# A conv-and-softmax-layer kernel: the prologue written anew, its first tiles in pairs, the tail's rows last

## The chip, the cores and the metric

The kernel runs on one core of a Trainium2 chip. The metric is the device time of one execution in microseconds (us). Engines: PE (TensorE: matmuls), PEld (its weight loads), ACT (ScalarE), DVE (VectorE), POOL (GpSimd), SP (SyncE, which here issues every DMA).

## The reference

```python
# x (8, 4160, 192), weight (8 heads, 7 taps); D = 192, 24 columns to a head
w = exp(weight - max(weight)); w = w / (sum(w) + 1e-9)
y[b, s, h, :] = sum_k w[h, k] * x[b, s + k - 6, h, :]      # zero before the start
# y as 33280 tokens of 192; w_in (192, 1024), w_out (1024, 192) are float64, g_ln (1024)
h = y @ w_in
e = exp(h - max(h)); sm = e / (sum(e) + 1e-9)
solu = h * sm
ln = (solu - mean(solu)) / sqrt(var(solu) + 1e-6) * g_ln
out = ln @ w_out
```

## The kernel before

Everything is one stream of 260 tiles of 128 tokens. x comes in 17 chunks (`Chunk`, L113): chunk 0 has 1024 rows (tiles 0 to 7), chunk 1 the other 1056 of the first half sequence (tiles 8 to 15), chunk 2 and the rest 2080 each. A chunk is loaded in windows of 112 rows with 16 of halo. PE convolves groups of heads with a banded tap matrix (`product`, L240, tiles pc), ACT and DVE write the result as two fp16 parts (`upper`, L293, `lower`, L302, tile y), SP turns them with transposing DMAs (`turn`, L335, y to yT), and `double` (L345) copies a third of yT to y2. A chunk has a power-of-two scale s, from squares that are summed (`sum_squares`, L164, tiles xj and xa), added over the partitions by a small PE matmul (`add_up`, L201) and turned into a power of two by four small DVE steps (`root_power`, L90). The scale's columns cv follow in `scale_steps` (L182).

A tile t then takes these steps: h in PSUM by ten matmuls 512 wide, yT against high and low parts of w_in (`emit_rows` L740, `emit_third` L748; two banks ph in rotation); its maximum on DVE (L772); exp on ACT (L779); the product e times h on DVE (L832, `emit_mul`, which frees ph); the fp16 high part on ACT (L840), the low part on POOL (L849), both transposed by one DMA (L851, pT); a square sum on ACT (L844); and, five tiles later, 24 matmuls 192 wide against ohi and olo, w_out's parts (L861, po), which DVE copies out (L868). For groups of up to eight tiles POOL makes the reciprocal roots (L912 to L922), the rows are multiplied by them on DVE or POOL (L931, L927, `run_rows` L1074), and SP stores pairs of rows (L940). The last three tiles are groups of one: a root of small steps each (L875 to L879) and the output straight from PSUM (L884, of).

The weights come as float64 words and are decoded by hand (`Words`, L483 on): exponent bits (L498) and mantissa bits (L503) cut on DVE, mantissa and low word joined to a float (L530 for w_in on DVE; L509, L521 and L524 for w_out on ACT and POOL), the exponent turned to a power of two on ACT (L536, `powers`), the sign put in on DVE (L539), and both multiplied (L546). w_in is worked on in two halves of 512 columns and a third part Z, the last 64 rows laid on all partitions. Its scale t_in is found from the largest absolute value (L515) and goes into the bias of `powers`, so that all later steps depend on it. whi is cast on ACT (L625, L643 to L648), wlo is the rest on DVE (L634). w_out's values are multiplied by g_ln and the powers in eight DVE steps (L695), its mean over the rows is made on PE (L704) and taken off on DVE (L714), ohi is cast on ACT (L718) and olo made on DVE (L723).

Each engine works its instructions off in the order in which the code issues them; nothing is reordered. What follows what is set by hand: `step(i)` (L1217) issues one tile and the parts of its neighbours, for tiles 0 to 7 and the last ones; `two_steps(i)` (L1146) issues a pair, for tiles 8 to 255. `chores` (L978) says, by fractions of a chunk's tiles, at which tile the next chunks are convolved (conv), opened, turned, doubled, loaded and summed. A run of matmuls of tile t + 2 waits until `emit_mul` of tile t has freed its buffer in PSUM.

## Time and profile before

| | us |
|---|---|
| median of three runs | 1205.08 (1202.68 to 1205.13) |
| the profiled execution | 1204.79 |
| its span in the trace | 1203.1 |
| PE busy in the span | 1158.8 (96%) |
| DVE, ACT, POOL busy | 1009.3, 946.3, 946.6 |
| start of tile 2, tile 8, tile 18 on PE | 37.47, 80.96, 137.72 |
| last instruction on an engine (L884) | 1199.98 |

A row of a timeline gives start, duration, engine, line, operation, output and inputs, and in brackets how long the engine stood idle before it and what ended that. A tail of "x2" says that two like instructions run together in one row, with the time from the first's start to the last's end. A row of the waits gives the total, the number and the longest. A row by lines gives busy time and mean ns of one.

### The profile page before, as it was taken

Reading aid. Unit: us, or ns where it says so; the run is one execution under the profiler, and the core shown is the slowest. Engines: PE = TensorE matmul, PEld = TensorE weight load, DVE = VectorE, ACT = ScalarE, POOL = GpSimd, SP = SyncE. Lnnn points to the kernel's source line nnn. Section 1 sums busy time; section 2 is a strip of 40 time slices with the busy share of each in tenths; the row PEclk is TensorE's granted clock in tenths of the full one; section 3 lists DMA queues with packets and bytes.
Section 4 is the critical chain, followed back from the end, with each engine's and each line's share of the span. In section 5 each row is a group of like instructions: output and inputs, shape, how many; then the busy total and the mean of one; then the engine's idle time right before and its main releaser. Section 6 shows DMA issues by size and latency. Waiting matters only on the chain.

```text
span 1203.1 us, 26422 instructions
## 1 busy us (share of the span) xinstructions
PE 1158.8 (96%) x9718; PEld 815.8 (68%) x9718; DVE 1009.3 (84%) x2172; ACT 946.3 (79%) x1518; POOL 946.6 (79%) x920
## 2 busy tenths in 40 slices
...
GB/s 246 96 168 127 164 207 193 211 201 202 209 193 208 187 211 197 202 196 185 217 175 218 179 199 208 194 200 185 213 205 206 194 189 155 170 171 191 183 156 153
DMA packets 727312, 227.48 MB, mean 189 GB/s; under 512 B 651454, under 2 KB 725582, under 8 KB 727182
## 3 DMA queue, kind: packets, MB, share of 16 engines
...
## 4 chain that ended last, share of the span: by engine, by line
PE 75%; POOL 8%; DVE 7%; issue 6%; ACT 2%; DMA 1%; POOLq 0%; ACTq 0%; SPq 0%; DVEq 0%
PE po L861 33%; PE ph L740 31%; POOL p L849 6%; PE pc L270 5%; PE ph L748 5%; DVE ph L772 1%; DVE e L832 1%; DMA yT<-y 1%; POOL t L921 1%; POOL raw L927 1%; ACT e L779 1%; DVE y L306 1%; DVE xa L171 0%; ACT y L297 0%; DMA pT<-p 0%
## 5 line engine op out<-in xcount | busy, mean ns | idle before, releaser
L849 POOL TENSOR_TENSOR p<-e,p 128x1024 f16<-128x1024 f32 x257 | 546.3, 2135 | 187.7 <-ACT p L840 187.6
L861 PE MATMUL po<-ohi,pT 128*128 128x192 f16 x4160 | 553.6, 246 | 4.3 <-DVE raw L931 4.3
L861 PEld LDWEIGHTS <-pT 128*128 128x128 f16 x6240 | 522.3, 98 | 37.9 <-DMA pT<-p 5.0
L861 PE MATMUL po<-olo,pT 128*128 128x192 f16 x2080 | 512.4, 246 | 1.5 <-DVE olo L723 1.5
L740 PE MATMUL ph<-whi,yT 128*128 128x512 f16 x1560 | 430.0, 385 | 21.2 <-DVE e L832 12.1
L779 ACT ACTIVATE e<-ph,sm 128x1024 f32<-128x1024 f32 x259 | 288.7, 1115 | 195.4 <-DVE ph L772 178.8
L772 DVE TENSOR_SCALAR_CACHE_REDUCE ph<-ph,cv 128x1024 f32<-128x1024 f32 x248 | 318.8, 1290 | 140.0 <-PE ph L748 92.3
L740 PEld LDWEIGHTS <-yT 128*128 128x128 f16 x2080 | 192.2, 99 | 271.3 <-issue 71.4
L832 DVE SCALAR_TENSOR_TENSOR e<-ph,cv,e 128x1024 f32<-128x1024 f32 x247 | 316.3, 1281 | 3.2 <-ACT e L779 1.3
L840 ACT CAST p<-e 128x1024 f16<-128x1024 f32 x259 | 269.5, 1040 | 21.3 <-DVE e L832 21.2
L844 ACT ACTIVATE sq<-e 128x1024 f32<-128x1024 f32 x259 | 273.7, 1057 | 3.9
L740 PE MATMUL ph<-wlo,yT 128*128 128x512 f16 x520 | 157.1, 384 | 2.5 <-DVE wlo L634 2.5
L225 POOL TENSOR_TENSOR xs<-xr,xs 128x960 f16<-128x960 f32 (+1 forms) x56 | 107.8, 1925 | 2.3
L868 DVE COPY raw<-po 128x192 f32<-128x192 f32 x257 | 90.6, 352 | 1.3 <-PE po L861 1.3
L306 DVE SCALAR_TENSOR_TENSOR y<-pc,y 112x480 f16<-112x480 f32 (+3 forms) x168 | 74.5, 471 | 17.0 <-ACT y L297 9.8
L748 PE MATMUL ph<-wlo,yT 64*128 64x512 f16 x268 | 82.8, 388 | 0.0
L748 PE MATMUL ph<-wlo,y 64*128 64x512 f16 x252 | 77.1, 385 | 0.0
L270 PE MATMUL pc<-xs,taps_hi 128*112 128x240 f16 (+1 forms) x448 | 72.9, 261 | 0.0
L171 DVE TENSOR_REDUCE xa<-xr 128x1 f32<-128x384 f32 x120 | 69.3, 618 | 0.0
L297 ACT ACTIVATE y<-pc 112x432 f16<-112x432 f32 (+5 forms) x140 | 63.3, 473 | 1.7 <-PE pc L270 0.6
L222 POOL TENSOR_SCALAR xr<-xr,s 128x960 f32<-128x960 f32 (+1 forms) x56 | 57.7, 1030 | 2.6 <-ACT xs L216 0.4
L270 PE MATMUL pc<-xs,taps_lo 128*112 128x240 f16 (+1 forms) x224 | 58.5, 261 | 0.0
...
## 6 DMA issues: line engine op xcount, KB each, us to landing
out_dram<-raw SPq DMA_DIRECT2D x128, 192.0 KB, 2.5
...
pT<-p SPq DMA_TRANSPOSE x259, 4.9
...
yT<-y SPq DMA_TRANSPOSE x99, 3.7
...
```

The source lines that it names most:

```text
L225: (2.1 * size + 0.2, lambda: pool.tensor_tensor(xl, r, h, ALU.subtract)),
L270: nc.tensor.matmul(o, tp[:, h + j, :], r, start=q == 0, stop=q == len(ops) - 1)
L740: nc.tensor.matmul(bank, lhs, w[:, r, n * 512 : (n + 1) * 512], start=start and j == 0, stop=stop and j == len(ops) - 1,)
L748: nc.tensor.matmul(banks_of(t)[n], y[q, t.off : t.off + P], wlo[q, 1, n * 512 : (n + 1) * 512], start=start, stop=not start,)
L772: dve.tensor_scalar(t.ph, t.ph, t.cv[:, 0:1], None, ALU.mult, ALU.min, accum_out=t.bias)
L779: act.activation(t.e, t.ph, AF.Exp, bias=t.bias, scale=-1.0, accum_out=grp.z[:, g : g + 1])
L832: dve.scalar_tensor_tensor(t.e, t.ph, t.cv[:, 3:4], t.e, ALU.mult, ALU.mult, accum_out=t.grp.s1[:, t.g : t.g + 1],)
L840: act.copy(t.p16[:, :, 0, :], t.halves)
L844: act.activation(junk, t.e, AF.Square, accum_out=t.grp.s2[:, t.g : t.g + 1])
L849: eng.tensor_tensor(t.p16[:, :, 1, :], t.halves, t.p16[:, :, 0, :], ALU.subtract)
L861: nc.tensor.matmul(t.po[:, 0:D], t.pT[:, a, :], w, start=j == 0, stop=j == len(ops) - 1)
L868: dve.tensor_copy(t.grp.raw[:, t.g, :], t.po[:, 0:D])
```

## The change

It has five parts. Lines of the changed kernel are shifted: `root_power` stays, L740 becomes L729, L772 L764, L832 L824, L849 L841, L851 L843, L931 L923.

w_in: its exponents become powers of two with a fixed bias, with no scale; ACT squares the powers and sums them (`squares`), PE adds the sums up, and t_in is made from that. Signs and values are done without t_in, which is applied where whi is copied (ACT, scale=t_in) and where wlo is made (DVE). `largest`, `floor`, `iq` and `bias_in` are gone. This is ACT in the prologue, before, where the powers of w_in and then whi wait on bias_in:

```order
12 L536 ACTIVATE e_in<-e_in,bias_in 128x512 x2
13 L297 ACTIVATE y_0_0_175<-pr_223,s_172 112x5x96
14 L297 ACTIVATE y_0_0_175<-pr_224,s_172 112x5x32
15 L297 ACTIVATE y_0_0_175<-pr_224,s_172 112x5x64
16 L625 CAST whi<-f_in 128x512 x2
17 L536 ACTIVATE e_in<-e_in,bias_in 128x512
18 L509 ACTIVATE raw_out<-raw_out 128x1536
19 L643 CAST whi<-f_in 64x512
20 L644 CAST whi<-f_in 64x512
21 L647 CAST whi<-f_in 64x512
22 L648 CAST whi<-f_in 64x512
```

and after, with rebias in place of bias_in, the squares at L464, and t_in among the inputs of whi:

```order
8 L177 ACTIVATE xj_2_169,xa_132<-xr_1_88 128x384
9 L481 ACTIVATE e_in<-e_in,rebias 128x512
10 L177 ACTIVATE xj_3_172,xa_132<-xr_1_88 128x576
11 L464 ACTIVATE oj_in_191,isq<-e_in 128x1024
12 L481 ACTIVATE e_in<-e_in,rebias 128x512
13 L305 ACTIVATE y_0_0_180<-pq,s_177 112x5x96
14 L305 ACTIVATE y_0_0_180<-pq,s_177 112x5x32
15 L305 ACTIVATE y_0_0_180<-pq,s_177 112x5x64
16 L464 ACTIVATE oj_in_209,isq<-e_in 128x512
17 L305 ACTIVATE y_0_0_180<-pr_219,s_177 112x5x96
18 L627 ACTIVATE whi<-f_in,t_in 128x512 x2
19 L635 ACTIVATE whi<-f_in,t_in 64x512 x4
```

The powers of w_in stand ahead of the first y rows of chunk 0 now (those of the first half two rows ahead of this piece), and the six copies of whi follow each other behind the scale.

w_out: the lows, the cast of the mantissas and the last product go to POOL, the factor g_ln to ACT (eight scalings of 192 columns), half of olo to POOL; t_out is in the averaging matrix `even` and in the subtraction of the mean. POOL before, from the end of its memsets on:

```order
15 L410 MEMSET even 128x128
16 L524 TENSOR_TENSOR f_out<-m_out,raw_out 128x1536
17 L849 TENSOR_TENSOR p_1_401<-e_338,p_1_401 128x2x512
18 L849 TENSOR_TENSOR p_2_446<-e_421,p_2_446 128x2x512
19 L849 TENSOR_TENSOR p_3_514<-e_443,p_3_514 128x2x512
20 L849 TENSOR_TENSOR p_4_581<-e_511,p_4_581 128x2x512
```

and after; raw_out, m_out, f_out and e_out are w_out's words, mantissas, values and powers:

```order
14 L416 MEMSET even 128x128
15 L450 TENSOR_SCALAR raw_out<-raw_out 128x1536
16 L198 TENSOR_SCALAR cv_178<-cv_178 128x1 x2
17 L456 TENSOR_SCALAR m_out<-m_out 128x1536
18 L469 TENSOR_TENSOR f_out<-m_out,raw_out 128x1536
19 L491 TENSOR_TENSOR f_out<-f_out,e_out 128x1536
20 L841 TENSOR_TENSOR p_0_322<-e_305,p_0_322 128x2x512
21 L841 TENSOR_TENSOR p_1_342<-e_320,p_1_342 128x2x512
22 L714 TENSOR_TENSOR olo<-f_out,ohi 128x768
23 L841 TENSOR_TENSOR p_2_409<-e_396,p_2_409 128x2x512
```

Five instructions for w_out stand where one stood, and the low halves begin with tile 0, which DVE made before.

Tiles 0 to 7 go in pairs: `first_two`, `second_two`, then `two_steps` from tile 4. Chunk 1's first two groups are convolved beside tiles 2 and 3 and kept (`early`), its sums of squares come behind tile 3's cast, and chunk 2's four first sums are squares on ACT.

Chunk 1 and 2 in `chores`: chunk 1's groups at tiles 4 and 5, chunk 2's groups one or two a pair over tiles 8 to 19, where they were two a pair over tiles 8 to 15. Chunk 2's transposes on SP, before, with y_2_0 its first ten windows:

```order
41 L851 DMA_TRANSPOSE pT_913<-p_10_910 128x16x128
42 L851 DMA_TRANSPOSE pT_923<-p_11_918 128x16x128
43 L336 DMA_TRANSPOSE yT_942<-y_2_0_751 128x10x112 x2
44 L150 DMA xr_1_973<-in_x_dram 128x5x192
45 L851 DMA_TRANSPOSE pT_1049<-p_12_1046 128x16x128
46 L851 DMA_TRANSPOSE pT_1063<-p_13_1054 128x16x128
47 L336 DMA_TRANSPOSE yT_942<-y_2_0_751 128x10x112
48 L349 DMA y_2_943<-yT_942 64x1120
49 L150 DMA xr_2_1112<-in_x_dram 128x5x192
```

and after:

```order
39 L843 DMA_TRANSPOSE pT_905<-p_10_902 128x16x128
40 L843 DMA_TRANSPOSE pT_915<-p_11_910 128x16x128
41 L150 DMA xr_1_947<-in_x_dram 128x5x192
42 L843 DMA_TRANSPOSE pT_1016<-p_12_1013 128x16x128
43 L843 DMA_TRANSPOSE pT_1027<-p_13_1022 128x16x128
44 L344 DMA_TRANSPOSE yT_1041<-y_2_0_757 128x10x112 x3
45 L357 DMA y_2_1042<-yT_1041 64x1120
46 L150 DMA xr_2_1083<-in_x_dram 128x5x192
```

All three transposes of its first ten windows follow pT of tile 13 now, where two stood one pair earlier.

The tail: `run_rows` is left out at tiles 257 to 259, so that rows of the groups at tile 240 and 248 are multiplied behind the last low parts (pl), and stores behind the last transposes. DVE before, with raw_15626 the rows of tiles 248 on and raw_15853 those of 252 on:

```order
1428 L931 TENSOR_SCALAR raw_15626,t_248_15318<-raw_15626,t_248_15319 128x192 x4
1429 L832 SCALAR_TENSOR_TENSOR e_15881,s_258_15862<-ph_15866,cv_13211,e_15881 128x1024
1430 L772 TENSOR_SCALAR ph_15929,sm_15943<-ph_15929,cv_13211 128x1024
1431 L868 COPY raw_15853<-po_15950 128x192
1432 L849 TENSOR_TENSOR p_258_15941<-e_15881,p_258_15941 128x2x512
1433 L800 SCALAR_TENSOR_TENSOR el_15945<-ph_15929,cv_13211,el_15945 128x512
1434 L800 SCALAR_TENSOR_TENSOR el_15946<-ph_15929,cv_13211,el_15946 128x512
1435 L808 TENSOR_TENSOR pl_15983<-el_15945,pl_15983 128x512
1436 L808 TENSOR_TENSOR pl_15986<-el_15946,pl_15986 128x512
1437 L931 TENSOR_SCALAR raw_15853,t_252_15531<-raw_15853,t_252_15532 128x192 x3
```

and after, where raw_15198 is tile 240's group, raw_15624 248's and raw_15851 252's:

```order
1384 L860 COPY raw_15851<-po_15936 128x192
1385 L841 TENSOR_TENSOR p_258_15927<-e_15873,p_258_15927 128x2x512
1386 L792 SCALAR_TENSOR_TENSOR el_15931<-ph_15915,cv_13209,el_15931 128x512
1387 L792 SCALAR_TENSOR_TENSOR el_15932<-ph_15915,cv_13209,el_15932 128x512
1388 L800 TENSOR_TENSOR pl_15969<-el_15931,pl_15969 128x512
1389 L800 TENSOR_TENSOR pl_15972<-el_15932,pl_15972 128x512
1390 L923 TENSOR_SCALAR raw_15198,t_240_14894<-raw_15198,t_240_14895 128x192 x4
1391 L923 TENSOR_SCALAR raw_15624,t_248_15316<-raw_15624,t_248_15317 128x192 x4
1392 L923 TENSOR_SCALAR raw_15851,t_252_15529<-raw_15851,t_252_15530 128x192 x3
```

The four rows of 248 that stood ahead of the product of tile 258, and four of 240 that DVE and POOL made earlier still, now stand on DVE with the last three, behind pl.

```diff
             self.sums, self.scaled = 0, False
             self.exact = ch < 3
-            self.peaks = ch > 1
+            self.peaks = 2 * self.np if ch < 2 else self.np if ch == 2 else 0
...
                 )
             self.sums += 1
-            if self.peaks:
+            if col >= self.peaks:
...
+        def lows(self, c, scale):
+            pool.tensor_scalar(
+                self.low[:, c].bitcast(F32), self.low[:, c], scale, 1.0,
+                ALU.mult, ALU.mult,
+            )
+
+        def floats(self, c):
+            pool.tensor_scalar(
+                self.m[:, c].bitcast(F32), self.m[:, c], 1.0, 1.0, ALU.mult, ALU.mult
+            )
+
+        def squares(self, c, to):
+
+            junk = sp.tile([P, F], F32, name=f"oj_{self.name}_{c.start}", tag="sq", bufs=1)
+            junk = junk.bitcast(F16)[:, 0 : c.stop - c.start]
+            act.activation(
+                junk, self.e[:, c].bitcast(F32), AF.Square, scale=2.0**20, accum_out=to
+            )
...
+        def powers(self, c):
+            act.activation(self.e[:, c], self.e[:, c], AF.Relu, bias=rebias, scale=8.0)
+
...
     got0 = [next(going)]
     c0.add_up()
     got0 += going
-    wi.largest(halves[0], floor[:, 0:1])
-    words(halves[0])
-    wi.largest(halves[1], floor[:, 1:2])
-    for f in chain0[1:-4]:
+    wi.squares(A, isq[:, 0:1])
+    valued(halves[0])
+    wi.exponents(Z)
+    for f in chain0[1:-3]:
         f()
-    wi.largest(Z, floor[:, 2:3])
...
-    tp = total(iq[:, 1:2], "wi")
+    wi.powers(Z)
+    valued(halves[1])
     for pc, hg in got0:
         c0.upper(pc, *hg)
-    for c in halves:
-        wi.powers(c, bias_in)
+    wi.mantissas(Z)
+    wi.join(Z)
+    wi.squares(Z, isq[:, 1:2])
     c0.open(0, None)
     settle(*spans0[0], got0)
...
+    got0 = [next(going)]
+
+    tp = total(isq, "wi")
+    got0 += going
+    dve.tensor_reduce(isq[:, 0:1], tp, AX.X, ALU.add)
+    for f in root_power(t_in, isq[:, 0:1], 2.0**26, 1e-12):
+        f()
+    c0.upper(*got0[0][:1], *got0[0][1])
     for c in halves:
-        valued(c)
-        act.copy(whi[:, 0, c], wi.f[:, c])
-    words(Z)
-    wi.powers(Z, bias_in)
+        act.activation(whi[:, 0, c], wi.f[:, c], AF.Copy, scale=t_in)
+    valued(Z)
...
+    def lower_in(to, of, hi, q=slice(0, P)):
+        dve.scalar_tensor_tensor(to, of, t_in[q], hi, ALU.mult, ALU.subtract)
...
-        gm = osq[:, 1:2]
-        dve.tensor_reduce(gm, gl, AX.X, ALU.max, apply_absolute_value=True)
-        dve.tensor_tensor(gm, gm, gm, ALU.mult)
-        dve.tensor_tensor(gm, gm, osq[:, 0:1], ALU.mult)
-        return total(gm, "wo", bank)
-
-    def out_root(tp):
-        for f in root_power(t_out, tp, 2.0**26, 1e-30):
+    def out_powers():
+
+
+        for j in range(NFC):
+            act.activation(
+                woe[:, j], woe[:, j], AF.Copy, scale=gl[:, j : j + 1]
+            )
+
+    def out_scale():
+        for f in root_power(t_out, total(osq, "wo"), 2.0**26, 1e-30):
             f()
+        dve.tensor_scalar(even, even, t_out, None, ALU.mult)
+
+    def out_root():
         inverse_power(o_inv, t_out, 1)
         dve.tensor_scalar(o_inv, o_inv, float(F) ** 0.5, None, ALU.mult)
-    def out_values():
-
-        wo.signs(W)
-        for j in range(NFC):
-            c = slice(j * D, (j + 1) * D)
-            dve.scalar_tensor_tensor(
-                wo.f[:, c], wo.f[:, c], gl[:, j : j + 1], wo.e[:, c].bitcast(F32),
-                ALU.mult, ALU.mult,
-            )
...
     def out_upper():
-        for cs in quarters:
-            c = slice(cs.start, cs.stop)
-            dve.tensor_tensor(
-                wof[:, c], wof[:, c],
-                mean[:, 0:D].unsqueeze(1).broadcast_to([P, len(cs), D]), ALU.subtract,
-            )
-            act.activation(ohi[:, c, :], wof[:, c], AF.Copy, scale=t_out)
+        for c in quarters:
+            dve.scalar_tensor_tensor(
+                wof[:, c], wof[:, c], t_out,
+                mean[:, 0:D].unsqueeze(1).broadcast_to([P, NFC // 2, D]),
+                ALU.mult, ALU.subtract,
+            )
+            act.copy(ohi[:, c, :], wof[:, c])
 
     def out_lower():
-        for cs in quarters:
-            c = slice(cs.start, cs.stop)
-            dve.scalar_tensor_tensor(
-                olo[:, c, :], wof[:, c], t_out, ohi[:, c, :], ALU.mult, ALU.subtract
-            )
+        for eng, c in zip((dve, pool), quarters):
+            eng.tensor_tensor(olo[:, c, :], wof[:, c], ohi[:, c, :], ALU.subtract)
 
...
+        if ch == 0:
+            put(0.5, 0.75, "conv", [(c1, hg) for hg in c1.groups()[2:]])
+            put(0.5, 1.0, "open", [c1])
+            turn(c1, c1.parts[0], 0.625, 0.7, 0.75)
+        elif ch == 1:
+            put(0.0, 0.7, "conv", [(c1, hg) for hg in c1.groups()[:4]])
+            put(0.5, 1.0, "open", [c1])
+            turn(c1, c1.parts[0], 0.5, 0.6, 0.75)
+            put(0.75, 1.0, "conv", [(c1, hg) for hg in c1.groups()[4:6]])
+        elif c1:
+            stage(c1, *((0.25, 0.95, 1.0) if ch == 2 else (0.0625, 0.875, 1.0)), c1.groups())
         if ch == 2:
-            turn(chunks[ch], chunks[ch].parts[1], 0.0, 0.4, 0.25)
+            put(0.0, 0.25, "conv", [(c0, hg) for hg in c0.groups()[6:]])
+            turn(c0, c0.parts[1], 0.19, 0.4, 0.4)
         if c2 and ch < 3:
-            sums(c2, *((0.45, 0.8), (0.0, 0.5), (0.0, 0.25))[ch])
+            sums(c2, *((0.5, 1.0), (0.0, 0.75), (0.0, 0.4))[ch])
         if c3:
             if ch:
                 put(*((0.0, 0.7) if ch > 2 else (0.25, 0.9 + 0.1 * (ch == 1))), "load",
...
+    def first_two():
+
+        t, u = prepare(0), prepare(1)
+        emit_two(t, u)
+        emit_max(t)
+        wo.powers(W)
+        emit_exp(t)
+        wo.signs(W)
+        wo.whole(W)
+        emit_max(u)
+        out_powers()
+        emit_mul(t)
+        emit_exp(u)
+        emit_hi(t)
+        settle_rest()
+        for c in chunks[3:4]:
+            for j in range(XR - sum(q.np for q in chunks[1:3])):
+                c.load(j)
+        wo.squares(W, osq)
+        wo.value(W, pool)
+        emit_mul(u)
+        emit_hi(u)
+        for q in (t, u):
+            emit_lo(q, pool)
+            q.split = True
+
+    def second_two():
+
+        t, u = prepare(2), prepare(3)
+        c = chunks[1]
+        emit_two(t, u)
+        emit_max(t)
+        out_scale()
+        early.append((c, *conv(c, c.groups()[0])))
+        out_mean()
+        emit_exp(t)
+        emit_square(tiles[0])
+        emit_max(u)
+        emit_exp(u)
+        out_upper()
+        numerators(t)
+        out_lower()
+        numerators(u)
+        for q in (t, u):
+            emit_lo(q, pool)
+        early.append((c, *conv(c, c.groups()[1])))
+        for j in range(c.np):
+            for h in c.halves(j):
+                c.sum_squares(*h)
+        follow(c, 3)
+        out_root()
+        for q in (tiles[1], t, u):
+            emit_square(q)
+
...
+        if i == NT:
+            last_sums(cur)
+        if not NT - 4 < i < NT:
+            run_rows(i)
...
-        if i >= NT - 2:
+        queue.run(2.0 if i < NT - 2 else 100.0)
+        if i >= NT - 1:
             run_rows(i)
             run_stores()
 
-    for i in range(PAIRED):
-        step(i)
-    for i in range(PAIRED, SINGLE, 2):
+    assert not any(chores(t.ch, t.k, t.n) for t in tiles[SINGLE:])
+    first_two()
+    second_two()
+    for i in range(4, SINGLE, 2):
         two_steps(i)
     for i in range(SINGLE, NT + DEPTH):
```

More of the change, by code (lines that the diff above doesn't have):

```diff
@@ L387 @@
     pool.memset(rebias, -916.0 * 2.0**23)
-    floor = cp.tile([P, 4], F32, name="floor")
-    pool.memset(floor, 2.0**-20)
     act.activation(rebias[0:1], rebias[0:1], AF.Copy)
@@ L417, with words, valued @@
+    wi, A, Z = Words(raw_in, "in"), slice(0, F), slice(F, 3 * F // 2)
+    HF = F // 2
+    halves = [slice(0, HF), slice(HF, F)]
+    def words(c):
+        wi.exponents(c)
+        wi.mantissas(c)
+        wi.join(c)
+    def valued(c):
+        wi.signs(c)
+        wi.value(c, dve)
     wtop = cp.tile([TJ, H], F32, name="wtop")
@@ L437 @@
     dve.tensor_tensor(b16[:, 1], bsum, b16[:, 0], ALU.subtract)
+    words(halves[0])
+    wi.powers(halves[0])
     taps = cp.tile([P, H, CW], F32, name="taps")
@@ L466 @@
         )
+    words(halves[1])
     for h in c0.halves(1):
         c0.sum_squares(*h)
+        if h[2] == 0:
+            wi.powers(halves[1])
     def split_taps(q):
@@ L549 @@
-    wi, A, Z = Words(raw_in, "in"), slice(0, F), slice(F, 3 * F // 2)
-    HF = F // 2
-    halves = [slice(0, HF), slice(HF, F)]
     t_in = cp.tile([P, 1], F32, name="t_in")
-    iq = cp.tile([P, 2], F32, name="iq")
-    bias_in = cp.tile([P, 1], F32, name="bias_in")
+    isq = cp.tile([P, 2], F32, name="isq")
     chain0 = c0.scale_steps()
@@ L996, in stage @@
             put(at[0], 1.0, "open", [c])
-            for part, *span in turns or zip(c.parts, at, [*at[1:], z]):
-                turn(c, part, *span)
+            for part, e, f in zip(c.parts, at, [*at[1:], z]):
+                turn(c, part, e, f)
         def sums(c, a, z):
@@ L1117 @@
     early = []
-    c1_sums = [
-        lambda h=h: chunks[1].sum_squares(*h)
-        for j in range(chunks[1].np) for h in chunks[1].halves(j)
-    ] if NCH > 1 else []
     def prepare(i):
@@ L1162, in two_steps @@
         got = []
+        held = early[:]
+        early.clear()
+        if held:
+            add_up(i + 1, held[-1][0].bank)
         for j in range(max(len(done), len(convs))):
@@ L1230, in step @@
         run_stores()
[L1231 to L1244 removed]
+        if i == NT - 1:
```

320 lines of the change are left out of this document (105 added, 215 removed).

## The prediction

> **What bounds the kernel now.** I read the page's first part, then busy time by stretch, then the waits of TensorE (PE) before 160 us, then the timelines of the places that they name.
>
> ```profile
> PE 1158.8 (96%) x9718; PEld 815.8 (68%) x9718; DVE 1009.3 (84%) x2172; ACT 946.3 (79%) x1518; POOL 946.6 (79%) x920
> ```
> ```profile
> 0.00:160.00 160.00, 125.10 (x844) 79.58 (x845) 128.47 (x291) 110.42 (x185) 68.78 (x57) 0.91 0.75 162
> 160.00:1170.00 1010.00, 1009.16 (x8653) 716.85 (x8652) 858.88 (x1814) 822.47 (x1310) 859.39 (x824) 1.00 1.03 194
> 1170.00:1203.10 33.10, 24.56 (x227) 19.42 (x224) 21.96 (x68) 13.44 (x25) 18.43 (x41) 0.95 0.79 156
> ```
>
> The columns are the stretch and its length, the busy time of PE, PEld, DVE, ACT and POOL, the granted clock, the DMA share and GB/s. From 160 to 1170 us PE idles 0.84 us in 1010, at full clock. The instructions of that stretch are the same before and after, so nothing is won or lost in it: what counts is how early PE enters it, and what follows it. Before 160 us PE idles 34.9 us, and its clock is below 1 for part of the rest; in the tail it idles 8.5.
>
> ```profile
> PE ph L740 <- DVE e L832: 10.3, 7, 4.2
> ...
> PE ph L740 <- DMA yT<-y: 5.6, 2, 3.3
> PE ph L740 <- ACT whi L625: 2.6, 2, 1.7
> ```
>
> Total, times, longest: PE waits for VectorE's mul (L832) to free a bank of h, twice for turned windows (yT), and at the start for w_in. The change touches all three.
>
> **1. w_in (tile 0 ends 4.1 us earlier).**
>
> ```profile
> 16.62 0.15 DVE L608 TENSOR_SCALAR bias_in<-t_in 128x1 f32<-128x1 int32 x1
> ...
> 22.98 0.69 DVE L539 SCALAR_TENSOR_TENSOR e_in<-raw_in,e_in 128x512 int32<-128x512 int32 x1 [0.19 <-ACT e_in L536]
> 23.71 0.69 DVE L546 TENSOR_TENSOR f_in<-f_in,e_in 128x512 f32<-128x512 f32 x1
> 26.35 0.62 ACT L648 CAST whi<-f_in 64x512 f16<-64x512 f32 x1
> ...
> 29.77 1.03 PE L740 MATMUL ph<-whi,yT 128*128 128x512 f16 x2
> ```
> ```profile
> L515 DVE TENSOR_REDUCE floor<-raw_in 128x1 f32<-128x512 f32 x3 | 2.0, 680 | 0.3 <-DMA raw_in<-in_moe_w_in_dram 0.3
> ```
> ```profile
> L306 DVE SCALAR_TENSOR_TENSOR y<-pq,s,y 112x320 f16<-112x320 f32 (+1 forms) x4 | 1.6, 457 | 0.0
> ```
>
> Before, the scale is there at 16.6, and the powers, signs and values that need it follow: the last copy of whi ends at 26.97 and tile 0 at 29.8, where tile 1 begins. After, the decode needs no scale, and DVE does it while it waits for DMA and PE. Only signs and value of the last third stay behind the scale. The scale itself comes later: ahead of it DVE now does two signs and two values (4 x 0.69 = 2.8), one more join (as wide, 0.7) and the four rows of y (1.6), and no longer three maxima (2.0) and some 0.7 of small steps: 16.6 + 5.1 - 2.7 = 19.0. Then 0.69 + 0.69 to 20.4 and four copies of 0.62 on ScalarE (ACT): the last whi at 22.85, 4.1 earlier. ACT's copies of the first two thirds run beside DVE's two steps. The lows (four as wide, from 20.4) end at 23.1, ahead of the two matmuls that read them last. Tile 0 ends at 25.7.
>
> **2. Tiles 0 to 7 in pairs (tile 8 starts 7.9 earlier).**
>
> ```profile
> 36.89 1.75 DVE L539 SCALAR_TENSOR_TENSOR e_out<-raw_out,e_out 128x1536 int32<-128x1536 int32 x1
> ```
> ```profile
> 37.47 1.01 PE L740 MATMUL ph<-whi,yT 128*128 128x512 f16 x2
> ...
> 44.86 0.60 PE L740 MATMUL ph<-whi,yT 128*128 128x512 f16 x2 [0.74 <-DVE e L832]
> ...
> 56.04 0.59 PE L740 MATMUL ph<-whi,yT 128*128 128x512 f16 x2 [4.19 <-DVE e L832]
> ...
> 80.96 0.59 PE L740 MATMUL ph<-whi,yT 128*128 128x512 f16 x2 [0.59 <-DVE e L832]
> ```
> ```profile
> 29.50 3.56 POOL L524 TENSOR_TENSOR f_out<-m_out,raw_out 128x1536 f32<-128x1536 f32 x1 [24.59 <-ACT m_out L521]
> 45.96 2.13 POOL L849 TENSOR_TENSOR p<-e,p 128x1024 f16<-128x1024 f32 x1 [12.90 <-ACT p L840]
> ```
>
> w_out's eight products leave DVE, for eight scalings on ACT and one whole-width product on GpSimd (POOL), which I price like POOL's whole-width sum, 3.56. POOL stood idle for 24.6 and 12.9 us around that sum, so its new work there is covered as long as nobody waits for it (rival a). I then walked the queues by durations of before, each instruction after the last of its inputs. Tile 1 ends at 29.75, with PE as slow as before. mul(0) and mul(1) end at 32.3 and 35.2 and free the two banks: tile 2 starts at 32.3 instead of 37.47. The scale of w_out comes at 39.8, its mean leaves PE at 42.9, mul(2) ends at 46.05. DVE's half of olo then meets POOL's half, and I add 1.3 for that (the row of olo below). mul(3) ends at 49.5; before, tile 4 waited for its bank until 56.04.
>
> From here ACT is last. Behind the cast of tile 3 (50.5) stand four sums of squares of chunk 1, three squares of tiles, then exp(4):
>
> ```profile
> L177 ACT ACTIVATE xj<-xr 128x384 f32<-128x384 f32 (+1 forms) x4 | 2.4, 603 | 0.1
> L177 ACT ACTIVATION_READ_ACCUMULATOR xj<-xr 128x1 f32 x4 | 0.7, 187 | 0.0
> ```
> ```profile
> 53.60 1.05 ACT L844 ACTIVATE sq<-e 128x1024 f32<-128x1024 f32 x1
> ```
>
> The four sums take 2.9 with their reads, to 53.4; three squares with theirs 3 x 1.15, exp(4) 1.2: 58.1. Tiles 4 and 5 then cost ACT another exp, two casts, six parts of y and two squares, some 8.5, and chunk 2's four sums (2.9) stand ahead of exp(6), which ends at 70.7. mul(6) and mul(7) follow, and the pair (8,9) starts at 73.1 against 80.96.
>
> **3. Chunks 1 and 2 (12.5 in all).**
>
> ```profile
> 84.35 1.74 PE L740 MATMUL ph<-whi,yT 128*128 128x512 f16 x4 [2.37 <-DMA yT<-y]
> ...
> 93.03 0.59 PE L740 MATMUL ph<-whi,yT 128*128 128x512 f16 x2
> ```
> ```profile
> 128.35 1.38 PE L740 MATMUL ph<-whi,yT 128*128 128x512 f16 x4 [3.28 <-DMA yT<-y]
> ...
> 137.72 0.60 PE L740 MATMUL ph<-whi,yT 128*128 128x512 f16 x2
> ```
> ```profile
> 117.66 5.70 SPq L851 DMA_TRANSPOSE pT<-p  x2
> 123.45 1.48 SPq L336 DMA_TRANSPOSE yT<-y  x1
> ```
> ```profile
> yT<-y SPq DMA_TRANSPOSE x99, 3.7
> ```
>
> Chunk 1's groups are convolved earlier, its windows are turned by about 74.5, and the wait at 84.35 goes: (10,11) starts at 82.2, 10.8 ahead of 93.03, and fewer groups per pair up to tile 15 hold that. Chunk 2's three transposes now all stand behind pT(13) on SP: 3 x 1.48, 3.7 to landing, and the copy of y2, behind a pT(13) issued at about 104 to 106, give 115 to 118. (16,17) starts at 111.8, 12.2 ahead, and waits for them about as long as it did; (18,19) starts at 124.4, 13.3 ahead. There stands one more group than before, 0.85. PE enters the filled stretch **12.5** earlier.
>
> **4. The tail (+0.3).**
>
> ```profile
> 1186.98 1.40 DVE L808 TENSOR_TENSOR pl<-el,pl 128x512 f16<-128x512 f32 x2
> 1190.16 0.41 DVE L931 TENSOR_SCALAR_CACHE_REDUCE raw<-raw,t 128x192 f32<-128x192 f32 x1 [1.79 <-POOL t L922]
> ...
> 1190.50 0.41 DVE L931 TENSOR_SCALAR_CACHE_REDUCE raw<-raw,t 128x192 f32<-128x192 f32 x1
> ```
> ```profile
> 1194.35 0.34 PE L861 MATMUL po<-ohi,pT 128*128 128x192 f16 x1 [4.31 <-DVE raw L931]
> ...
> 1194.58 0.15 DVE L875 TENSOR_TENSOR t<-z 128x1 f32<-128x1 f32 x1
> ...
> 1199.98 0.48 DVE L884 TENSOR_SCALAR of<-po,t,o_inv 128x192 f32<-128x192 f32 x1 [0.91 <-PE po L861]
> ```
>
> Eight rows (L931) now follow the last lows instead of going ahead: 8 x 0.334 = 2.7 from 1188.38, while DVE idled 1.79 there; the three rows behind them end 0.89 later, and the first of the three last roots starts at 1195.47 (1194.58 + 0.89). PE gets the last pT some 4 us sooner, since two stores go behind it and the lows of tile 258 come sooner. But then DVE's chain of three roots is last, and the last output (L884, at 1199.98) ends 0.3 later. Bounds: -1 (the last lows come sooner too) to +0.9.
>
> **Sum.** -12.5 + 0.3 = -12.2. The profiled execution took 1204.79 (span 1203.1 and 1.7 around it), 0.3 under the median of 1205.08: 1192.6, and by the median **1193**. Own range 1190 to 1196: 2 each way for the slow clock of the first tiles and ACT's order at 50 to 70 us, 1 for the tail. What a measurement can tell from no change is about 0.2%, 2.4 us.
>
> **A rule against it.** Rows where DVE reads two SBUF operands while POOL works:
>
> ```profile
> L1138 DVE TENSOR_TENSOR xa<-xa x15: 166/1145/2066, 74.6 to 980.6; 128x8 f32<-128x8 f32 x15
> ```
> ```profile
> L723 DVE SCALAR_TENSOR_TENSOR olo<-f_out,t_out,ohi x2: 1004/1576/2149, 46.8 to 48.8; 128x768 f16<-128x768 f32 x2
> ```
>
> Shortest, median, longest in ns: a product of eight columns takes 0.17 at best and up to 2.07, about a POOL low half (2.13). The olo beside that low half took 2.15, the other 1.00. The Trainium skill, page "SBUF — State Buffer", section "Who interferes with whom", calls the port pair that both engines share an exclusive lock; by that rule, the trace agrees.
>
> **Rivals.**
>
> (a) *POOL goes first at w_out* (0.18). POOL's whole-width sum and DVE's signs of w_out (1.75) come due within 0.5 us of each other near 27 us; I let DVE go first. If POOL does, DVE stands still behind it, +2.85 by the walk, and +1.9 more if the cast that moved to POOL costs as much as the sum: 1196 to 1198.
>
> (b) *The lead is lost at chunk 2* (0.10). If each of the three yT takes SP as long as each pT beside it (2.85, not 1.48) and lands as much later, (16,17) waits 6 us longer: 1199.
>
> (c) *PE's clock is up from the first tiles* (0.08). Before, it was not:
>
> ```profile
> 27.00:34.00 7.00, 6.99 (x17) 1.85 (x17) 5.23 (x14) 5.62 (x6) 3.56 (x1) 0.55 0.84 227
> ```
>
> PE is filled for 7 us at 0.55, and two matmuls that take 0.60 at 44.86 take 1.03 at 29.77. At the full clock tile 1 would take 2.4 instead of 4.1, and the end of tile 0 a little less too, about -2 in all: 1190.5. The Trainium skill, page "TensorE: Matmul & The Clock Gate", section "What's actually happening", puts the full rate after some 3.4 us of sustained work; this row disagrees with that.
>
> (d) *DVE doesn't set the end* (0.04): PE's 4 us in the tail count, about 1189.
>
> (e) *Slower: such a stop at each new meeting of DVE and POOL* (0.08). POOL's work on w_out goes from one instruction to five, and each can stand in the way of a DVE instruction with two SBUF operands: the lows (3.56 at most) of the joins and signs of w_in, two more (7.1) of the signs of w_out, a low half and the half of olo (3.7) of DVE's olo, low halves (2 x 1.9) of the small products of chunk 1 and 2. That is 18.2, of which 1.3 is in my sum: 1193 + 16.9 = 1210. It decides from three quarters of that price on. For it: the two rows above. Against it: in the walk most of these do not meet.
>
> That the change does nothing is ruled out by the rows at 16.62 and 84.35: what caused these waits isn't there any more.
>
> **Chances.** Forecast 0.52, (a) 0.18, (b) 0.10, (c) 0.08, (d) 0.04, (e) 0.08. Faster by over 0.2% holds the forecast, (a), (c), (d) and 0.07 of (b); 0.03 of (b) and 0.02 of (e) lie within 0.2%: 0.89, 0.05, 0.06. The range goes down to 1187, past (c) and (d), and up to 1200.5, past (a) and most of (b); (e) and the end of (b) are left out, some 0.12.
>
> **What would show it.** Right: the last copy of whi ends near 23, tile 8 starts near 73 and tile 18 near 124, PE doesn't wait for yT at tile 8, in the tail DVE stands without idle from the last lows to the roots. Wrong: signs of w_out over 3 us; ACT idle between 50 and 70 us; a wait for yT at tile 16 of over 6 us; PE idle past 160 us.

## The result and the profile after

The changed kernel takes 1220.36 us (median of 4 runs, 1218.67 to 1220.9) and the kernel before 1204.63 in the same comparison: ratio 1.0131, 95% interval 1.0114 to 1.0149. It is slower by 1.3%, where 1193 was forecast. The profiled execution took 1218.67 with a span of 1217.0, 13.9 more than before.

The page's busy times, and busy time by stretch (columns as in the prediction; the last stretch ends with the span):

```profile
PE 1157.2 (95%) x9718; PEld 814.0 (67%) x9718; DVE 1007.7 (83%) x2119; ACT 950.9 (78%) x1536; POOL 961.6 (79%) x956
```
```profile
0.00:160.00 160.00, 120.22 (x834) 77.58 (x835) 123.58 (x250) 115.38 (x202) 80.31 (x69) 0.90 0.73 159
160.00:1170.00 1010.00, 1002.69 (x8567) 710.55 (x8565) 854.35 (x1786) 812.84 (x1296) 853.27 (x836) 1.00 1.03 194
1170.00:1217.00 47.00, 34.33 (x321) 25.87 (x318) 29.74 (x84) 22.66 (x40) 28.02 (x53) 0.95 0.66 137
```

PE has less done by 160 us (120.2 busy us, 125.1 before), and the stretch taken to be full idles 7.3 us. The starts on PE of the first matmul of h of some pairs say where the time went:

| tile | before | after | difference | forecast |
|---|---|---|---|---|
| 2 | 37.47 | 38.05 | +0.6 | 32.3 |
| 4 | 56.04 | 52.70 | -3.3 | |
| 6 | 69.17 | 73.13 | +4.0 | |
| 8 | 80.96 | 82.91 | +2.0 | 73.1 |
| 10 | 93.03 | 91.06 | -2.0 | 82.2 |
| 16 | 124.04 | 124.80 | +0.8 | 111.8 |
| 18 | 137.72 | 136.71 | -1.0 | 124.4 |
| 24 | 165.10 | 166.13 | +1.0 | |
| 26 | 173.97 | 182.73 | +8.8 | |
| 40 | 235.21 | 245.41 | +10.2 | |
| 256 | 1166.04 | 1177.04 | +11.0 | 1153.5 |

Hardly any lead is left at tile 18, 7.7 us go in the one pair (24,25), and 2.9 more in the tail: from the end of h of tile 259 to the end of the span are 23.9 us (from 1193.03 on), 21.1 before (from 1182.02 on). These starts come from one execution each. In new_tail_alone (run 3), whose code up to the tail is that of before, tile 8 starts at 78.68 and tile 18 at 136.49, so a difference of 2 us in this table says little by itself.

**The prologue.** Timeline of after:

```profile
13.77 0.69 DVE L484 SCALAR_TENSOR_TENSOR e_in<-raw_in,e_in 128x512 int32<-128x512 int32 x1 [1.58 <-ACT oj_in L464]
...
16.89 1.57 POOL L450 TENSOR_SCALAR raw_out<-raw_out 128x1536 f32<-128x1536 uint32 x1 [12.02 <-DMA raw_out<-in_moe_w_out_dram]
...
16.98 2.00 DVE L491 TENSOR_TENSOR f_in<-f_in,e_in 128x512 f32<-128x512 f32 x1
...
30.49 3.47 POOL L469 TENSOR_TENSOR f_out<-m_out,raw_out 128x1536 f32<-128x1536 f32 x1
...
30.79 4.79 DVE L484 SCALAR_TENSOR_TENSOR e_out<-raw_out,e_out 128x1536 int32<-128x1536 int32 x1
```

The signs of w_in write over the powers that ACT is still squaring (L464), so DVE waits 1.58. A value of 512 columns (0.69 alone) takes 2.00 beside POOL's low words, and w_out's signs take 4.79 beside POOL's whole-width sum (1.75 before): Both end behind POOL's instruction (18.98 against 18.46, 35.58 against 33.96), and each is longer by about what was left of POOL's when it began (1.31 of 1.48, 3.04 of 3.17). The second is rival (a), and its price of 2.85 was close (3.04).

**Tiles 6 to 25.** PE's timeline of after, three of its rows:

```profile
71.42 1.91 PE L278 MATMUL pc<-xr,taps 128*112 128x120 f32 x8 [4.34 <-DVE y L314]
...
124.80 1.01 PE L729 MATMUL ph<-whi,yT 128*128 128x512 f16 x2 [3.94 <-issue]
...
173.13 0.60 PE L737 MATMUL ph<-wlo,y 64*128 64x512 f16 x1 [4.79 <-DMA y<-yT]
...
174.09 1.03 PE L729 MATMUL ph<-whi,yT 128*128 128x512 f16 x2
```

Three waits of over 3.9 us: for a buffer of the convolution, for yT at tile 16, and for y2 at tile 25. SP's timeline of after around the last two:

```profile
113.62 5.15 SPq L843 DMA_TRANSPOSE pT<-p  x2
118.82 5.21 SPq L344 DMA_TRANSPOSE yT<-y  x3
...
156.38 1.85 SPq L344 DMA_TRANSPOSE yT<-y  x1
...
160.02 6.94 SPq L843 DMA_TRANSPOSE pT<-p  x2
167.01 3.12 SPq L344 DMA_TRANSPOSE yT<-y  x2
...
170.88 0.50 SPq L357 DMA_DIRECT2D y<-yT  x1
```

The copy y2<-yT needs only the block that went out at 156.38. It stands at tile 22 in the code, behind two more blocks at tiles 20 and 21, and those behind two pT; so it leaves at 170.88 for a reader at 168.3. Before, with the copy at tile 20, it left at 157.32, and PE did not wait for y2. SP's timeline of before, then PE's at tile 25:

```profile
157.32 0.48 SPq L349 DMA_DIRECT2D y<-yT  x1
```
```profile
166.93 0.39 PE L748 MATMUL ph<-wlo,y 64*128 64x512 f16 x1
```

**The tail.** SP's and DVE's timelines of after:

```profile
1198.74 3.56 SPq L801 DMA_TRANSPOSE pT<-pl  x2
1202.35 7.23 SPq L932 DMA_DIRECT2D out_dram<-raw  x7
```
```profile
1199.30 0.41 DVE L923 TENSOR_SCALAR_CACHE_REDUCE raw<-raw,t 128x192 f32<-128x192 f32 x1
...
1205.68 0.36 DVE L860 COPY raw<-po 128x192 f32<-128x192 f32 x1 [2.63 <-DMA out_dram<-raw]
...
1213.88 0.48 DVE L876 TENSOR_SCALAR of<-po,t,o_inv 128x192 f32<-128x192 f32 x1 [0.66 <-POOL t L871]
```

The rows follow the last lows at 0.33 us each, as forecast. Then the copy of tile 255's rows waits 2.63 us for the stores of a group three before it, whose buffer it takes: the change has put them last on SP.

### The profile page after: what moved, and what is told of

The parts are those of the page before. It is cut to its first block, busy times and chain, and to the rows that moved or that the text cites. A ratio compares the mean times of both kernels' runs of the same rounds, so it can differ in the third digit from the quotient of the medians.

```text
span 1217.0 us, 26425 instructions
## 1 busy us (share of the span) xinstructions
PE 1157.2 (95%) x9718; PEld 814.0 (67%) x9718; DVE 1007.7 (83%) x2119; ACT 950.9 (78%) x1536; POOL 961.6 (79%) x956
## 4 chain that ended last, share of the span: by engine, by line
PE 80%; DVE 7%; POOL 4%; issue 4%; ACT 2%; DMA 2%; SPq 0%; POOLq 0%; DVEq 0%; ACTq 0%
PE po L853 36%; PE ph L729 34%; PE ph L737 5%; PE pc L278 5%; POOL p L841 2%; DVE e L824 1%; DVE ph L764 1%; DMA pT<-p 1%; DVE cvm L339 1%; ACT e L771 1%; DMA raw_in<-in_moe_w_in_dram 1%; DVE cvm L338 1%; POOL xs L233 1%; DVE raw L923 0%; DVE y L314 0%
## 5 line engine op out<-in xcount | busy, mean ns | idle before, releaser
L841 POOL TENSOR_TENSOR p<-e,p 128x1024 f16<-128x1024 f32 x258 | 548.8, 2136 | 171.3 <-ACT p L832 171.0
L729 PE MATMUL ph<-whi,yT 128*128 128x512 f16 x1560 | 429.7, 385 | 21.9 <-DVE e L824 9.9
L764 DVE TENSOR_SCALAR_CACHE_REDUCE ph<-ph,cv 128x1024 f32<-128x1024 f32 x248 | 319.0, 1291 | 144.4 <-PE ph L737 94.3
L729 PEld LDWEIGHTS <-yT 128*128 128x128 f16 x2080 | 192.1, 99 | 271.3 <-issue 70.9
L824 DVE SCALAR_TENSOR_TENSOR e<-ph,cv,e 128x1024 f32<-128x1024 f32 x247 | 316.4, 1281 | 4.4 <-ACT e L771 2.5
L832 ACT CAST p<-e 128x1024 f16<-128x1024 f32 x259 | 269.5, 1040 | 21.4 <-DVE e L824 20.8
L729 PE MATMUL ph<-wlo,yT 128*128 128x512 f16 x520 | 157.4, 384 | 0.1
L860 DVE COPY raw<-po 128x192 f32<-128x192 f32 x257 | 90.6, 353 | 4.1 <-DMA out_dram<-raw 2.6
L314 DVE SCALAR_TENSOR_TENSOR y<-pc,y 112x480 f16<-112x480 f32 (+3 forms) x168 | 74.5, 471 | 17.4 <-ACT y L305 10.1
```

The costliest lines, as they stand in the source:

```text
L729: nc.tensor.matmul(bank, lhs, w[:, r, n * 512 : (n + 1) * 512], start=start and j == 0, stop=stop and j == len(ops) - 1,)
L764: dve.tensor_scalar(t.ph, t.ph, t.cv[:, 0:1], None, ALU.mult, ALU.min, accum_out=t.bias)
L824: dve.scalar_tensor_tensor(t.e, t.ph, t.cv[:, 3:4], t.e, ALU.mult, ALU.mult, accum_out=t.grp.s1[:, t.g : t.g + 1],)
L832: act.copy(t.p16[:, :, 0, :], t.halves)
L841: eng.tensor_tensor(t.p16[:, :, 1, :], t.halves, t.p16[:, :, 0, :], ALU.subtract)
L860: dve.tensor_copy(t.grp.raw[:, t.g, :], t.po[:, 0:D])
```

## The experiments

All are of the changed kernel unless said otherwise. Times are medians, each against the kernel before on the same chip (1203.5 to 1204.0).

**1. turn_sooner**: chunk 2's second part turned whole at tile 19, doubled at tile 20.

```diff
-            turn(c0, c0.parts[1], 0.19, 0.4, 0.4)
+            turn(c0, c0.parts[1], 0.19, 0.2, 0.25)
```

> The changed kernel with one number altered: the second part of the third chunk is turned by three transposes in a row at tile 19 and doubled at tile 20, instead of tiles 19 to 21 and 22. Theory (the wait of pair 24 is for these transposes and the copy of y2, which SP issues behind the pT of tiles 20 and 21): the 4.8 us wait before tile 25's first matmul and the slow clock behind it go, pair 26 starts about 7 us sooner against pair 24 (8.9 instead of 16.6 us after it), and the time falls by 6 to 8 us, to 1212 to 1214. Rival (SP and the DMA queues are the limit, and the transposes only take their place elsewhere): the pT of tiles 20 and 21 come as much later, PE waits for them some pairs on, and the time stays within 2 us of 1220.

1210.93, ratio 1.006 (1.0045 to 1.0075). SP's timeline of it:

```profile
156.01 4.85 SPq L344 DMA_TRANSPOSE yT<-y  x3
...
162.26 0.47 SPq L357 DMA_DIRECT2D y<-yT  x1
```

PE does not wait for y2, and (26,27) starts at 174.96, 7.8 sooner. This one line is worth 9.4 us by the medians and 8.6 by the profiled executions (tile 256), more than the 6 to 8 expected.

**2. old_tail**: the order of the tail as before.

```diff
-        if i == NT:
-            last_sums(cur)
-        if not NT - 4 < i < NT:
-            run_rows(i)
+        run_rows(i)
...
+        if i == NT:
+            last_sums(cur)
...
-        if i >= NT - 1:
+        if i >= NT - 2:
```

> The changed kernel with the tail's order of before (rows at tiles 257 to 259, stores from tile 258 on). Theory (the postponed stores hold a buffer of rows that the copy of the next group needs; DVE stands 2.6 us behind it): the wait of the copy for a store goes, from the last product's pair at tile 258 to the end it takes 21 us instead of 24, the time falls by 2.6 to 3, to 1217.5. Rival (DVE's chain of rows and roots is longer by itself, the wait for the store lies beside it): at most 0.5 us.

1215.94, 1.0106 (1.0087 to 1.0126). That is 4.4 less than after by the medians, more than the theory's 2.6 to 3. From the end of h to the end of the span are 20.4 us, 3.5 less, and the copy's row on DVE has no wait:

```profile
1201.41 0.35 DVE L860 COPY raw<-po 128x192 f32<-128x192 f32 x1
```

**3. new_tail_alone**: the kernel before, with the same edit the other way round.

> The kernel before with only the tail's new order. Theory: the same wait for a store appears in it, 2.5 to 3 us more, 1207.5. The prediction's own reckoning: 0.3 more (between 1 less and 0.9 more). Rival (the tail costs only behind the changed prologue): no difference.

1207.82, 1.0031 (1.0018 to 1.0044); the tail takes 23.9. The wait comes with that order alone; DVE's timeline, then SP's:

```profile
1194.80 0.36 DVE L868 COPY raw<-po 128x192 f32<-128x192 f32 x1 [2.58 <-DMA out_dram<-raw]
```
```profile
1191.48 7.21 SPq L940 DMA_DIRECT2D out_dram<-raw  x7
```

**4. join_on_dve**: w_out's join on DVE in one step, in place of POOL's three (lows, floats, whole).

```diff
-    wo.lows(W, 2.0**-32)
...
+    wo.join(W)
...
-    wo.floats(W)
...
-        wo.whole(W)
```

> The changed kernel with w_out's words joined to floats in one DVE step, as w_in's are, instead of three POOL steps (lows, cast, sum). Theory (DVE steps with two SBUF operands stand still while such a POOL step runs): the value of w_in's second half takes 0.69 instead of 2.00, signs of w_out 1.75 instead of 4.79, the join costs 2.0 before the first maximum; t_in comes 1.3 sooner, tile 2 starts 2 to 3 us sooner, and pair 24 as much sooner if nothing else holds it: 1217 to 1218.5. Rival (these two steps are slow for another reason, such as their own operands' form): they stay at 2.0 and 4.8, the join comes on top, 1222.

1215.84, 1.0103 (1.0088 to 1.0119). DVE's timeline:

```profile
16.78 0.69 DVE L491 TENSOR_TENSOR f_in<-f_in,e_in 128x512 f32<-128x512 f32 x1
...
30.26 1.75 DVE L484 SCALAR_TENSOR_TENSOR e_out<-raw_out,e_out 128x1536 int32<-128x1536 int32 x1
```

Both instructions have their old length again. Tile 2 starts at 34.80 (38.05), and 4.5 us are won at the end by the medians (3.2 at tile 256 by the profiled executions), though the join now takes 1.76 us of DVE.

**5. held_at_once** (one execution): where a pair of tiles keeps two groups of the convolution, both are written out in the next pair, not one of them, so that both buffers come free.

```diff
-            later = held[1:] + [(c, *conv(c, hg)) for c, hg in convs]
+            later = [(c, *conv(c, hg)) for c, hg in convs]
...
-        for c, pc, hg in held[:1]:
+        for c, pc, hg in held:
```

> The changed kernel, with the second convolution group of chunk 1 that was kept from tile 3 taken out of PSUM right behind the first, ahead of exp(5), instead of behind tile 5's cast. Theory (PE's 4.3 us at 67 us are the fourth group waiting for that buffer, and everything behind it on PE with it): the wait shrinks to under 1 us and tile 6 starts 3 us sooner, about 70 instead of 73.1; the end gains up to 3. Rival (ACT, which does the extra y parts ahead of exp(5), is the limit there): tile 6 within 1 us of 73.1.

1218.97, span 1217.3 (1217.0 without the edit). Tile 6 starts at 67.72 instead of 73.13, so the buffer was the wait. But tile 8 starts at 81.18 instead of 82.91, tile 10 at 91.72 instead of 91.06, and nothing is won at the end. The lead ends at the transposes of chunk 1, which come no sooner. PE's timeline of this run at tile 8, then SP's:

```profile
81.18 1.03 PE L729 MATMUL ph<-whi,yT 128*128 128x512 f16 x2 [4.59 <-DMA yT<-y]
```
```profile
70.98 4.68 SPq L843 DMA_TRANSPOSE pT<-p  x2
75.77 4.61 SPq L344 DMA_TRANSPOSE yT<-y  x3
```

The three blocks of chunk 1 stand on SP behind pT of tiles 4 and 5, which go out at 70.98 here and at 70.45 in after. In after PE came to tile 8 later than the blocks did, and so did not wait for them.

**6. squares_by_thirds** (one execution): squares of w_in after each power, ahead of the next signs, with a third column in isq.

```diff
+    wi.squares(halves[0], isq[:, 0:1])
...
+            wi.squares(halves[1], isq[:, 1:2])
...
-    wi.squares(A, isq[:, 0:1])
```

> The changed kernel, with the squares of w_in's powers taken by ACT right behind each half's powers, three columns instead of two. Theory (signs write over the powers, so DVE stands 1.6 us at 13.8 until ACT has squared both halves): that wait goes, t_in comes 1.3 to 1.6 sooner and so does the first copy of whi (22.4 before this). Rival (the landing of w_in's second half and the taps set the pace there): t_in within 0.5 us of 22.2.

1217.77, span 1216.0. Timeline of DVE:

```profile
12.42 0.68 DVE L484 SCALAR_TENSOR_TENSOR e_in<-raw_in,e_in 128x512 int32<-128x512 int32 x1
...
17.12 1.97 DVE L475 SCALAR_TENSOR_TENSOR f_in<-raw_in,m_in 128x512 f32<-128x512 uint32 x1
```

The wait of 1.58 is gone, but then another instruction meets POOL's lows (1.97 for 0.69), and t_in comes 0.95 sooner, no more.

**7. five_repairs**: 1, 2, 4, 5 and 6 together.

> The changed kernel with all of it: sooner turn of the third chunk's second part, old tail, w_out joined on DVE, squares by thirds, both kept groups taken out at once. Theory (five separate losses): pair 26 starts 2 to 7 us ahead of the kernel before (after had 8.8 behind), the tail lasts 21 us, the time is 1198 to 1203, a little faster than before. Rival (the third chunk's first transposes, three behind pT of tile 13, take the whole lead at tile 16): pair 18 starts within 2 us of the kernel before, the time is 1203 to 1207.

1203.06, 0.9998 (0.9987 to 1.0008): the same as before. Tile 8 starts 4.4 ahead of before and tile 18 5.9 ahead; at tile 256 1.1 is left. PE still waits 4.53 at tile 8, for chunk 1's yT, and 3.93 at tile 16.

**8. six_repairs**: as 7, and chunk 2's first four groups convolved at tiles 8 to 11, their windows turned with the pair (10,11), behind pT(11), instead of with (12,13), behind pT(13).

```diff
-            put(0.0, 0.7, "conv", [(c1, hg) for hg in c1.groups()[:4]])
-            put(0.5, 1.0, "open", [c1])
-            turn(c1, c1.parts[0], 0.5, 0.6, 0.75)
+            put(0.0, 0.5, "conv", [(c1, hg) for hg in c1.groups()[:4]])
+            put(0.375, 1.0, "open", [c1])
+            turn(c1, c1.parts[0], 0.375, 0.45, 0.5)
```

> As five_repairs, and the third chunk's first four groups are convolved at tiles 8 to 11, two a pair, opened and turned by tile 11 and doubled at tile 12, one pair sooner. Theory (the 3.9 us before tile 16 are its three transposes behind pT of tile 13): the wait before tile 16 goes, the lead there is kept, 1194 to 1199. Rival (two groups a pair at tiles 8 to 11 cost on ACT and DVE what the wait cost): within 1 us of five_repairs.

1197.16 (1196.87 to 1199.52), 0.9948 (0.9932 to 0.9964): faster than both kernels. Busy time to 160 us, and PE's timeline at tile 16 and ahead of tile 20:

```profile
0.00:160.00 160.00, 129.67 (x925) 84.81 (x926) 129.80 (x274) 123.64 (x218) 82.98 (x80) 0.98 0.81 172
```
```profile
116.28 0.59 PE L729 MATMUL ph<-whi,yT 128*128 128x512 f16 x2
...
136.78 0.36 PE L573 MATMUL tph<-b,shift 20*128 20x224 f16 x2 [1.69 <-DVE y L314]
137.07 0.61 PE L729 MATMUL ph<-whi,yT 128*128 128x512 f16 x2
```

There is no wait at tile 16; tile 18 starts at 125.77, 11.95 ahead of before. The tail's order is that of before. PE still waits 4.40 at tile 8 for chunk 1's yT. Of the lead 9.3 are left at tile 20, behind the wait of 1.69, 8.0 at tile 40 and 7.2 at tile 256.

**9. spread_undone**: chunk 2 convolved and turned at the tiles of before.

```diff
-            put(0.0, 0.7, "conv", [(c1, hg) for hg in c1.groups()[:4]])
-            put(0.5, 1.0, "open", [c1])
-            turn(c1, c1.parts[0], 0.5, 0.6, 0.75)
-            put(0.75, 1.0, "conv", [(c1, hg) for hg in c1.groups()[4:6]])
+            put(0.0, 1.0, "conv", [(c1, hg) for hg in c1.groups()])
+            put(0.375, 1.0, "open", [c1])
+            turn(c1, c1.parts[0], 0.375, 0.625, 0.75)
...
-            put(0.0, 0.25, "conv", [(c0, hg) for hg in c0.groups()[6:]])
-            turn(c0, c0.parts[1], 0.19, 0.4, 0.4)
+            turn(c0, c0.parts[1], 0.0, 0.4, 0.25)
```

> The changed kernel with the third chunk's schedule of before (eight groups two a pair at tiles 8 to 15, two transposes behind pT of tile 11 and the third behind that of tile 13, second part turned at tiles 16 to 20, doubled at 20); all else as changed. Theory (the spread schedule is what costs at tile 24, and moves the first part's last transposes late): the wait at tile 24 goes and the one before tile 16 shrinks to 1 to 3 us, the time falls by 8 to 11, to 1209 to 1212. Rival (the prologue's five POOL steps are the main loss, as the prediction's slower rival had it): under 4 us of fall.

1210.91, 1.006 (1.0044 to 1.0077). The time lies in the range of the theory, but the wait did not go as it said: the pair (24,25) waits here too, in tile 25, for the third block. PE's timeline, then SP's:

```profile
169.71 1.45 PE L729 MATMUL ph<-whi,yT 128*128 128x512 f16 x4 [2.95 <-DMA yT<-y]
```
```profile
166.52 1.33 SPq L344 DMA_TRANSPOSE yT<-y  x1
```

**10. spread_alone**: the kernel before with only the new places of chunk 2.

> The kernel before with only the third chunk's spread schedule, prologue, single tiles and tail untouched. Theory: waits at tile 16 (all three transposes behind pT of tile 13) and at tile 24 (second part behind pT of tile 21): tile 26 comes 6 to 10 us later, 1210 to 1214. Rival (the spread costs only behind the changed prologue, whose pairs run closer): 1203 to 1206.

1213.14, 1.0084 (1.0069 to 1.0099). PE's waits in it, at tile 16 and at tile 25:

```profile
PE ph L740 <- issue: 4.2, 1, 4.2
...
PE ph L748 <- DMA y<-yT: 3.7, 1, 3.7
```

Without any new prologue the spread costs 8.1 us at tile 256, so the wait at tile 25 is its own and not the prologue's. At tile 18 the run is level with before (137.76 against 137.72), which waits 3.28 for yT at tile 16 itself; 6.1 of the 8.1 go in the pair (24,25).

**11. six_and_tile16**: as 8, with chunk 2's last group a tile sooner.

```diff
-            put(0.0, 0.25, "conv", [(c0, hg) for hg in c0.groups()[6:]])
+            put(0.0, 0.125, "conv", [(c0, hg) for hg in c0.groups()[6:]])
```

> As six_repairs, with the third chunk's last group convolved beside tile 17 instead of tile 18. Theory (PE's 1.7 us at 135 us wait for this group's buffer before the taps' matmuls): the wait goes, tile 20 comes 1.5 us sooner, 1195 to 1197. Rival (the wait moves to the pair ahead): as six_repairs, 1197.

1201.09, 0.998 (0.9971 to 0.9989), 4 us over six_repairs: the theory fell. (In the profiled executions 1.5 of it is there at tile 10 already, which the edit does not touch; 2.6 come behind it.) The wait on DVE's y came a pair sooner and was longer, and PE's clock fell behind it. PE's timeline, and the stretch after the wait:

```profile
130.60 0.46 PE L573 MATMUL tph<-b,shift 20*128 20x224 f16 x2 [2.69 <-DVE y L314]
130.99 1.03 PE L729 MATMUL ph<-whi,yT 128*128 128x512 f16 x2
```
```profile
131.00:134.00 3.00, 3.00 (x9) 1.00 (x8) 1.46 (x3) 2.96 (x7) 3.00 (x3) 0.50 0.65 142
```

**12. prologue_and_pairs**: 9 and 2 together, so that the new prologue, the pairs and the new places of chunk 1 and of the sums of squares are left.

> The changed kernel with the third chunk's schedule and the tail of before: what is left of the change is the prologue and the pairs from tile 0 on. Theory (three separate losses that add up): spread_undone stood 3.8 us behind before ahead of the tail, and the old tail took 0.7 less than before's, so 1206 to 1208, 2 to 4 slower than before; the prologue that was to gain 8 to 10 gives nothing by tile 26. Rival (the parts hide each other, and the prologue alone gains what was forecast): under 1200.

1207.07, 1.003 (1.0019 to 1.0041). Tile 18 starts 2.4 ahead of before, tile 26 3.3 behind. SP's timeline, then POOL's:

```profile
161.35 5.23 SPq L843 DMA_TRANSPOSE pT<-p  x2
166.63 1.71 SPq L344 DMA_TRANSPOSE yT<-y  x1
```
```profile
137.18 1.07 POOL L230 TENSOR_SCALAR xr<-xr,s 128x960 f32<-128x960 f32 x1
```

PE waits 5.0 us for yT, half of it at tile 25. In before the third block goes out at 164.99 and PE does not wait. POOL's halving of chunk 3 starts at 126.61 there, at 137.18 here (its sums are spread further), and POOL's low halves, on which pT waits, stand between its steps. That last link is read from the trace; no run moves it alone.

Parts measured apart add up: 8.1 for the spread (run 10) + 2.8 in the tail (run 3) + 3.5 for prologue and pairs (run 12, at tile 256) = 14.4, against 13.9.

## Why the prediction was wrong

**Bound (right idea, wrong use).** PE's idle time before 160 us and in the tail was the place to look. Wrong was that the stretch from 160 us on neither wins nor loses because its instructions are the same. Their order on SP is not: the change moves a transpose and a copy between tiles 19 and 22, whose reader stands at 168 us.

**Step 1, w_in (forecast -4.1, came to -0.3).** The scale came at 22.36, not 19.0. Missed were the 1.58 that the signs wait for ACT's squares (run 6 took it away) and POOL's low words beside a value, +1.31 (run 4 took that away); the other 0.5 is not traced. The casts of whi took what was said, ending at 26.67 (26.97 before); tile 0's first matmul waits 3.41 for them.

**Step 2, tiles 0 to 7 (forecast -7.9, came to +2.0).** Rival (a) happened. The walk also left out that the products of convolution take buffers in PSUM: DVE writes out only the first of two kept groups in a pair, and PE waits 4.34 for the other's buffer, 5.4 us at tile 6 by run 5. And it had chunk 1's windows turned by about 74.5, where the blocks leave SP from 76.12 to 80.54 in after. Tile 8 comes 9.8 later than forecast; five_repairs brings 6.3 of that back, and the rest stands behind its wait of 4.53 for these blocks.

**Step 3, chunks 1 and 2 (forecast -12.5, came to -1.0 at tile 18 and +11.0 at tile 256).** By the profiled executions the forecast is off by 26.1 (1218.67 against 1192.6): 9.8 of that had gone by tile 8, in steps 1 and 2, 1.7 more by tile 18, 12.0 went between tiles 18 and 256, and 2.6 in the tail. So step 2 failed, and this step failed by more: it took the lead at tile 18 for the gain at the end. The walk stopped there and never priced the other moved line, the second part's copy at tile 22 for a reader at tile 25: 8.6 to 9.4 us (run 1).

Up to tile 18 this step did better. That the wait at tile 8 for yT would go came true in after, but by luck: PE is late there, and in runs 5, 7 and 8, where it comes sooner, it waits 4.4 to 4.6. The wait at tile 16, for chunk 2's blocks behind pT(13), was to last about as long as before (3.28), and lasts 3.94. It is not tied to a fixed time: in runs 4 and 7 tile 16 starts 3.2 and 5.2 sooner, behind a wait of 4.0 and 3.9. What that place on SP costs is shown by six_repairs, which turns at tile 11, has no wait there and takes 5.9 us less than five_repairs.

**Step 4, the tail (forecast +0.3, came to +2.9).** Rows and roots have the lengths that were forecast. The mis-sized term is the stores: they were counted as making way for pT, not as holders of a buffer that a later copy needs. Runs 2 and 3 show 3.5 and 2.8.

**Rivals.** (a) came, at about the price given for it. (b) did not come: the three yT ahead of tile 16 take SP 1.74 each (5.21 in all), not 2.85, and the wait is 0.7 longer than before, not 6. (c) did not come either: from 20 to 30 us the clock is 0.54, in the row

```profile
20.00:30.00 10.00, 5.63 (x12) 1.29 (x13) 8.77 (x21) 6.56 (x9) 1.40 (x3) 0.54 0.63 160
```

The prediction's own row for (c), 7 us filled at 0.55 in before, shows less than it says. In the clock's record of that trace the 0.50 lasts from 23.09 to 33.33, three steps of 3.41, and PE, idle from 26.24 to 27.01, fills only the last of them whole; the full clock follows. So the row does not speak against a release after some 3.4 us of sustained work.

(d) did not come: the end hangs on DVE's late copy and the roots behind it (L860 at 1205.68, L876 at 1213.88). (e), the one slower rival, put 16.9 us on meetings of DVE and POOL; giving back w_out's join brings 3.2 to 4.5. The result lies on its side, by another mechanism: the places of DMAs on SP, and a buffer. Of the signs listed as wrong, three came: w_out's signs over 3 us, PE idle past 160, and ACT idle between 50 and 70 us (5.0 of the 20). The wait at tile 16 stayed under 6 us.

What stays open: between tiles 18 and 24 after loses 2.0, with a wait of 1.69 for DVE's y ahead of tile 20, and run 11 only made that wait longer. Between tiles 26 and 256 after loses 2.2 more in steps of 0.3 to 0.8 us, and six_repairs 2.4 of its lead; no run tells these apart. The last of the steps, 0.8 at tile 154, is there in new_tail_alone too, whose code there is that of before, so it is not put down to the change.
